# The second factor's way back from sums and differences of conjugate pairs, in 32x32 tiles of TensorE

## The chip, the cores and the metric

The kernel runs on one core of a Trainium2 chip. A core has TensorE (PE in the profile, with PEld for its weight loads), VectorE (DVE), ScalarE (ACT), GpSimd (POOL), SyncE (SP, which only issues transfers here) and 16 DMA engines. TensorE's 128x128 array can be used as smaller tiles that work side by side; it writes its results to PSUM, in banks of 128 partitions x 512 fp32 values. The metric is the time of one execution on the device in microseconds (us), the median of several runs.

## The reference, cut to what matters

```python
x: (8, 3008, 256);  filt_r, filt_i: (1505, 256)          # all fp32
X = np.fft.rfft(x, axis=1)                               # along the 3008 positions
Y = X * (filt_r + 1j * filt_i)[None]
y = np.fft.irfft(Y, n=3008, axis=1).astype(np.float32)   # (8, 3008, 256)
x = y.reshape(8 * 3008, 256)
h = x @ w_in                                             # 256 -> 2048
g = np.where(h > 0, h, np.exp(np.minimum(h, 0)) - 1)
out = g @ w_out                                          # 2048 -> 256
```

## The kernel before

The transform of length 3008 is done in two factors, 64 (with the twiddles in its tables) and 47. Rows n1 and 47 - n1 go together, so that 24 pairs stand for the 47. For each batch the stages are: `a_unit`, the first factor; `b_unit`, the way there of the second factor and the product with the filter; `bi_unit`, the way back of the second factor; `n_unit`, the way back of the first factor. Between the stages data go through DRAM (`z_write`, `z_read`, `y_write`, `y_read`) to be laid out anew. `b_unit` and `bi_unit` work in eight steps g of four values k2 each.

```python
def tile_mm(ps, table, k, rhs, special):
    for u, w, v in ((0, 1, 1), (1, 1, 0)) if special else ((0, 2, 0),):
        for n, r in enumerate(rhs):
            nc.tensor.matmul(ps[:, u:u + w, :], table[k, v, :], r[k, u:u + w, :], ...)   # L298

def b_unit(b, g, f=None, gb=gb, pq=None, between=None):
    ...
    (i0, re), (i1, im) = (bank(n) for n in ("psr", "psi"))
    for o, a in ((0, 0), (64, 2)):
        for ps, k in ((re, LO), (im, HI)):       # LO, HI: partitions 0-47 and 64-111
            tile_mm(ps[o:o + 64], gb, k, [t[:, a:a + 2, :]], g == 0 and a == 0)
    ...
    nc.vector.tensor_tensor(out=sr, in0=re, in1=f[:, 0], op=ALU.mult)
    nc.vector.tensor_tensor(out=si, in0=re, in1=f[:, 1], op=ALU.mult)
    nc.vector.scalar_tensor_tensor(out=p, in0=im, scalar=-1.0, in1=f[:, 1], op0=ALU.mult, op1=ALU.mult)
    nc.vector.tensor_tensor(out=q, in0=im, in1=f[:, 0], op=ALU.mult)
    banks.extend((i0, i1))
    ...                                          # batch 0 stops here: both parts go to bi_unit
    nc.gpsimd.tensor_tensor(out=sr, in0=sr, in1=p, op=ALU.add)
    nc.gpsimd.tensor_tensor(out=si, in0=si, in1=q, op=ALU.add)

def bi_unit(b, g):
    ...
    (i0, pa), (i1, pb) = (bank(n) for n in ("pva", "pvb"))     # for b > 0
    for o, table, sv in ((0, gr, s[0]), (64, gi, s[1])):
        for ps, k in ((pa, LO), (pb, HI)):
            tile_mm(ps[o:o + 64], table, k, sv, g == 0 and k == LO)
    nc.scalar.activation(out=t[:, 0:2, :], in_=pa, func=AXT.Copy)   # L337
    nc.scalar.activation(out=t[:, 2:4, :], in_=pb, func=AXT.Copy)   # L338
```

The two dense matrix products are done by a scheme that takes seven products of half-size blocks in place of eight. `up_steps` (L417, into the banks phs, pha, phd) and `down_steps` (L499, into four banks po of their own) are seven steps each of two matmuls of 128 rows and 128 columns. The main loop goes through 8 x 6 x 4 = 192 items ("quads"), and puts the units of the transform of the next batch into them, 24 quads to a batch:

```python
banks = [0, 1, 2, 3]                             # PSUM banks shared by all stages but po
PER = 24
for g in range(NG + 2):                          # NG = 8; t is the batch's first quad
    s = t + 9 + g
    if g >= 2: at(s, 1, bi_unit, b, g - 2)       # place 1: at the end of quad s
    if g < NG: at(s, 1, b_unit, b, g)
    if g >= 2: at(s, 1, y_write, b, g - 2)
...
for m, (s, place) in enumerate(((20, 0), (25, 1), (29, 1), (32, 0), (36, 0), (40, 0))):
    ...  at(t + s, place, n_unit, b, m)
...
for i in range(-PER, len(items) + 3):
    for k in "UUDUDDU": ...                      # one up or down step each
    for fn, a in plan.get((i, 0), ()): fn(*a)    # place 0
    for k in "DUUDUDD": ...
    ...                                          # the tails of the up and down steps
    for fn, a in plan.get((i, 1), ()): fn(*a)    # place 1
```

Batch 0 goes through the transform in an opening part of its own, ahead of the loop, with tables of its own (`once`).

Of the kernel before, what the change touches and what calls it, by code (L numbers as in the profile page):

```python
# [41 lines left out]
def _make_tables():  # L42
# [51 lines left out]
    gr[0:24, 1, 0:24], gr[24:48, 1, 24:48] = m0 * c0.T, m3 * c3.T  # L94
    gi[0:24, 1, 24:48], gi[24:48, 1, 0:24] = -m0 * s0.T, -m3 * s3.T
    lie = np.concatenate([2 * np.arange(24), 2 * np.arange(24) + 1])
    gb[:, :, lie] = gb[:, :, :48].copy()
# [6 lines left out]
    once = np.stack([np.eye(P), gf.reshape(P, P)], 1)  # L104
    return [t.astype(np.float32) for t in (ta, tn, np.stack([gb, gr, gi], 1), tf, once)]

# [7 lines left out]
def kernel(  # L114
# [10 lines left out]

    ta_d, tn_d, gs_d, tf_d, once_d = [
        nc.inline_tensor(t, name=n + "_t").ap()
        for t, n in zip(_make_tables(), ("ta", "tn", "gs", "tf", "once"))
    ]

    def pool(name, bufs, **kw):
        return ctx.enter_context(tc.tile_pool(name=name, bufs=bufs, **kw))
# [7 lines left out]
    t2p = pool("t2p", 2)  # L140
    sp = pool("sp", 2)
    qp = pool("qp", 1)
    t3p = pool("t3p", 2)
    t4p = pool("t4p", 2)
# [6 lines left out]

    gs = glob.tile([P, 3, 2, 64], FP32, name="gs")
    gb, gr, gi = (gs[:, i] for i in range(3))

# [3 lines left out]
    edges = glob.tile([P, 2], FP32, name="edges")  # L158
    fd = fdp.tile([NG, 2, 48, 2, 2, D], FP32, name="fd")

    xs, tas, tns, t1s, t2s, ss, t3s, t4s, zs, yds, ys, g_of, po_of, cs_, sds = ({} for _ in range(15))
# [127 lines left out]

    def f_read(b, g, t=None):  # L290
        t = fbufs[(b * NG + g) % FBUFS] if t is None else t
        for a, r in enumerate((LO, HI)):
            nc.gpsimd.dma_start(t[r].rearrange("p c u d -> p (c u d)"), fd[g, a].rearrange("q c u d -> q (c u d)"))

    def tile_mm(ps, table, k, rhs, special):
# [3 lines left out]

    def b_unit(b, g, f=None, gb=gb, pq=None, between=None):  # L300
        t = t2s.pop((b, g))
        f = fbufs[(b * NG + g) % FBUFS] if f is None else f
        (i0, re), (i1, im) = (bank(n) for n in ("psr", "psi"))
        for o, a in ((0, 0), (64, 2)):
            for ps, k in ((re, LO), (im, HI)):
                tile_mm(ps[o:o + 64], gb, k, [t[:, a:a + 2, :]], g == 0 and a == 0)
        if between:
            between()
        sr, si = (sp.tile([P, 2, D], FP32, tag=n, name=n) for n in ("sr", "si"))
        p, q = pq or (qp.tile([P, 2, D], FP32, tag=n, name=n) for n in ("sp", "sq"))  # L310

        nc.vector.tensor_tensor(out=sr, in0=re, in1=f[:, 0], op=ALU.mult)
        nc.vector.tensor_tensor(out=si, in0=re, in1=f[:, 1], op=ALU.mult)
        nc.vector.scalar_tensor_tensor(out=p, in0=im, scalar=-1.0, in1=f[:, 1], op0=ALU.mult, op1=ALU.mult)  # L314
        nc.vector.tensor_tensor(out=q, in0=im, in1=f[:, 0], op=ALU.mult)
        banks.extend((i0, i1))
        if b == 0:

            ss[b, g] = [sr, p], [si, q]
            return  # L320
        nc.gpsimd.tensor_tensor(out=sr, in0=sr, in1=p, op=ALU.add)  # L321
        nc.gpsimd.tensor_tensor(out=si, in0=si, in1=q, op=ALU.add)
        ss[b, g] = [sr], [si]

    def bi_unit(b, g):
        s = ss.pop((b, g))
        t = t3s[b, g] = t3p.tile([P, 4, D], FP32, tag="t3", name="t3")
        if b == 0:

            pa, pb = (psO.tile([P, 2, 256], FP32, tag="po%d" % i, name="po%d" % i)  # L330
                      for i in ((0, 1) if g > 2 and g % 2 else (2, 3)))
        else:
            (i0, pa), (i1, pb) = (bank(n) for n in ("pva", "pvb"))
        for o, table, sv in ((0, gr, s[0]), (64, gi, s[1])):
            for ps, k in ((pa, LO), (pb, HI)):
                tile_mm(ps[o:o + 64], table, k, sv, g == 0 and k == LO)
        nc.scalar.activation(out=t[:, 0:2, :], in_=pa, func=AXT.Copy)  # L337
        nc.scalar.activation(out=t[:, 2:4, :], in_=pb, func=AXT.Copy)  # L338
        if b > 0:
            banks.extend((i0, i1))  # L340

    def y_write(b, g, queues=(nc.sync, nc.sync)):
        if g == 0:
            yds[b] = yd.tile([K2, 96, D], FP32, tag="yd", name="yd")
        t = t3s.pop((b, g))
        for a, r in enumerate((LO, HI)):
            queues[a].dma_start(yds[b][4 * g:4 * g + 4, 48 * a:48 * a + 48, :].rearrange("u r d -> r u d"), t[r])

# [285 lines left out]
    def f_arrange():  # L634

        for c, src in enumerate((filt_r, filt_i)):
# [14 lines left out]
            nc.gpsimd.dma_start(fd[0, 0, 47:48, c, 1, :], raw(src, 4, [[D, 1], [1, D]]))  # L651

    with tc.manual_schedule():


        with tc.tile_pool(name="boot", bufs=1) as bp:
            ff = bp.tile([P, NG, 2, 2, D], FP32, name="ff")
            once = bp.tile([P, 2, P], FP32, name="once")
            eye, gf = once[:, 0], once[:, 1].rearrange("p (v q) -> p v q", v=2)
            pq = [bp.tile([P, 2, D], FP32, name="pq%d" % i) for i in range(2)]  # L660
            zt[0] += [bp.tile([P, 16 * ROWS], FP32, name="zt%d" % i) for i in range(2)]
# [50 lines left out]
            for g in range(NG):  # L712
                f_read(0, g, ff[:, g])
                if 3 <= g < 5:
                    w_fetch(g + 7)
# [6 lines left out]
            for g in range(NG + 2):  # L722
                back = (lambda g=g: bi_unit(0, g - 2)) if g >= 2 else None
                if g < NG:
                    b_unit(0, g, ff[:, g], gf, pq if g % 2 else None, back)
                else:
                    back()
                if g < 4:
                    t_first(g + 4)
                if g < 5:  # L730
                    w_float(g + 7)
                if g < 3:
                    w_join(g + 7)
                    w_split(g + 8)
                if g == 2:
                    w_split(11)
                if g >= 2:
                    y_write(0, g - 2, (nc.sync, nc.scalar if g == NG + 1 else nc.sync))
                if g == 7:
                    w_join(10)  # L740
                    w_join(11)
                    w_split(12)
                    w_split(13)
# [19 lines left out]
        PER = 24  # L763
        plan = {}

        def at(quad, place, fn, *a):
            plan.setdefault((quad, place), []).append((fn, a))
# [5 lines left out]
        for c in range(2, XBUFS):  # L773
            at(c - 2, 0, x_load, 1, c)
        for i, f in enumerate(fbufs):
            at(3 + i, 1, nc.vector.memset, f, 0.0)
        for b in range(B):
            t = (b - 1) * PER
            if b > 0:
                for c, s in enumerate((1 if b == 1 else 0, 2, 3, 4, 6, 7)):  # L780
                    at(t + s - 1, 0, x_unit, b, c)
                    at(t + s, 0, a_unit, b, c)
                    nb, nxt = (b, c + XBUFS) if c + XBUFS < NXC else (b + 1, c + XBUFS - NXC)
                    if nb < B:
                        at(t + s, 0, x_load, nb, nxt)
                    at(t + s, 0, z_write, b, c)
                for g in range(NG + 2):
                    s = t + 9 + g
                    if g >= 2:
                        at(s, 1, bi_unit, b, g - 2)  # L790
                    if g < NG:
                        at(s, 1, b_unit, b, g)
                    if g >= 2:
                        at(s, 1, y_write, b, g - 2)
                for g in range(NG):
                    s = t + 7 + g
                    at(s, 1, f_read, b, g)
                    at(s, 1, z_read, b, g)
            for m, (s, place) in enumerate(((20, 0), (25, 1), (29, 1), (32, 0), (36, 0), (40, 0))):
                if b > 0 or m > 0:  # L800
                    at(t + s - (1 if m == 0 else 2), 0, tn_read, b, m)
                    at(t + s - (1 if m == 0 else 2), 0, y_read, b, m)
                    at(t + s, place, n_unit, b, m)
                at(t + PER + 4 * m + 5, 0, c_unit, b, m)
                at(t + PER + 4 * m + 6, 0, o_unit, b, m)

        items = [(b, m, q) for b in range(B) for m in range(6) for q in range(4)]
        for i in range(-PER, len(items) + 3):
            ups, up_tail = up_steps(*items[i]) if 0 <= i < len(items) else ((), None)
            downs, down_tail = down_steps(*items[i - 1]) if 1 <= i <= len(items) else ((), None)  # L810
            ups, downs = list(ups), list(downs)
            for k in "UUDUDDU":
                s = ups if k == "U" else downs
                if s:
                    s.pop(0)()
            for fn, a in plan.get((i, 0), ()):
                fn(*a)
            for k in "DUUDUDD":
                s = ups if k == "U" else downs
                if s:  # L820
                    s.pop(0)()
# [38 lines left out]
```

## Time and profile before

| what | value |
|---|---|
| time, median of 3 runs | 2641.85 us (2640.01 to 2643.4) |
| span of the profiled execution | 2639.1 us |
| instructions | 37322 |
| TensorE clock granted, mean | 0.995 of full speed |
| first matmul of the main loop | 97 us after the span's start |
| DMA | 202.85 MB, mean 77 GB/s |

The busy share of an engine is the time in which it had an instruction running. Line numbers (L298) are those of the kernel before; a line in a helper, as L298, gathers all its callers, so tiles (psr, psi of `b_unit`; pva, pvb of `bi_unit`) tell them apart. The chain of work that ended last is followed back from the last instruction, and tells which engine's work the end had to wait for. Matmuls are pipelined, and the ends that the profile gives them are modelled; the distance of two starts is the surer measure.

### The profile page before, as it was taken

Reading aid. Unit: us, or ns where it says so; the run is one execution under the profiler, and the core shown is the slowest. Engines: PE = TensorE matmul, PEld = TensorE weight load, DVE = VectorE, ACT = ScalarE, POOL = GpSimd, SP = SyncE. Lnnn points to the kernel's source line nnn. Section 1 sums busy time; section 2 is a strip of 40 time slices with the busy share of each in tenths; the row PEclk is TensorE's granted clock in tenths of the full one; section 3 lists DMA queues with packets and bytes.
Section 4 is the critical chain, followed back from the end, with each engine's and each line's share of the span. In section 5 each row is a group of like instructions: output and inputs, shape, how many; then the busy total and the mean of one; then the engine's idle time right before and its main releaser. Section 6 shows DMA issues by size and latency. Waiting matters only on the chain.

```text
span 2639.1 us, 37322 instructions
## 1 busy us (share of the span) xinstructions
PE 2589.8 (98%) x13508; PEld 2208.4 (84%) x13508; DVE 1843.4 (70%) x3203; ACT 1508.0 (57%) x2622; POOL 236.7 (9%) x298
## 2 busy tenths in 40 slices
PE   5899999999999999999999999999999999999998
PEld 4688789887898888987889888988789887898887
DVE  6876766677666776677667676776767677666666
ACT  7655556555555555655555555555555555555554
POOL 5001200021000210002100020001200011000000
PEclk9999999999999999999999999999999999999999
DMA  9643313422233331424213341134321333110010
GB/s 292 151 104 88 86 34 76 114 75 75 52 92 79 90 73 39 103 73 103 72 37 87 93 111 45 39 92 105 98 50 43 81 78 81 38 41 19 22 28 17
DMA packets 224456, 202.85 MB, mean 77 GB/s; under 512 B 127586, under 2 KB 191090, under 8 KB 224272
## 3 DMA queue, kind: packets, MB, share of 16 engines
q1 hardware_dynamic: 211632, 166.70, 25.3%
q0 software_dynamic: 11184, 33.04, 4.9%
q8 instruction: 107, 1.75, 0.3%
q10 hardware_dynamic: 1456, 0.72, 0.1%
q14 instruction: 77, 0.63, 0.1%
HBM read 128.52 MB, written 74.97 MB: 77 GB/s over the span
## 4 chain that ended last, share of the span: by engine, by line
PE 97%; DMA 1%; DVE 1%; ACT 1%; issue 0%; SPq 0%; DVEq 0%; ACTq 0%
PE po L499 43%; PE phs L417 25%; PE phd L417 12%; PE pha L417 6%; PE psn L369 3%; PE pva L298 2%; PE psr L298 2%; PE psa L209 2%; DMA xc<-in_x_dram 1%; PE po L298 0%; PE psi L298 0%; PE pvb L298 0%; PE po L270 0%; DMA t<-yd 0%; PE psa L250 0%
## 5 line engine op out<-in xcount | busy, mean ns | idle before, releaser
L499 PE MATMUL po<-g,wo 128*128 128x256 f32 (+1 forms) x5376 | 1296.7, 375 | 0.0
L499 PEld LDWEIGHTS po<-g,wo 128*128 128x128 f32 x5376 | 1015.0, 190 | 129.5 <-issue 15.0
L428 ACT ACTIVATE g<-phs 128x512 f32<-128x512 f32 (+1 forms) x576 | 339.0, 589 | 842.7 <-PE phs L417 842.1
L425 DVE TENSOR_TENSOR g<-phd,g 128x512 f32<-128x512 f32 (+1 forms) x384 | 259.6, 676 | 457.2 <-ACT e L435 278.4
L435 ACT ACTIVATE e<-e 128x512 f32<-128x512 f32 (+1 forms) x768 | 477.3, 622 | 24.4
L417 PE MATMUL phs<-y,wi 128*128 128x256 f32 (+1 forms) x1536 | 395.2, 380 | 0.0
L417 PE MATMUL phs<-ys,wi 128*128 128x256 f32 (+1 forms) x1536 | 387.7, 375 | 0.7 <-ACT g L428 0.6
L439 DVE SCALAR_TENSOR_TENSOR g<-e,g 128x512 f32<-128x512 f32 (+1 forms) x576 | 387.1, 672 | 0.0
L434 ACT ACTIVATE e<-g 128x512 f32<-128x512 f32 (+1 forms) x576 | 352.7, 612 | 32.8 <-DVE g L425 28.1
L417 PEld LDWEIGHTS phs<-y,wi 128*128 128x128 f32 x1536 | 285.0, 190 | 83.2 <-ACT t L337 34.1
L417 PEld LDWEIGHTS phs<-ys,wi 128*128 128x128 f32 x1536 | 291.4, 190 | 34.6 <-ACT g L428 1.7
L439 DVE SCALAR_TENSOR_TENSOR g<-e,phs 128x512 f32<-128x512 f32 (+1 forms) x192 | 130.0, 677 | 138.6 <-ACT e L435 138.6
L417 PE MATMUL phd<-ys,wi 128*128 128x256 f32 (+1 forms) x768 | 193.8, 375 | 0.8 <-DVE g L425 0.8
L434 ACT ACTIVATE e<-phs 128x512 f32<-128x512 f32 (+1 forms) x192 | 113.0, 589 | 141.5 <-PE phs L417 140.6
L417 PE MATMUL phd<-y,wi 128*128 128x256 f32 (+1 forms) x768 | 193.7, 375 | 0.0
L417 PE MATMUL pha<-y,wi 128*128 128x256 f32 (+1 forms) x768 | 193.7, 375 | 0.0
L321 POOL TENSOR_TENSOR sr<-sr,sp 128x512 f32<-128x512 f32 x56 | 71.2, 1271 | 1246.3 <-DVE sp L314 1246.3
L417 PEld LDWEIGHTS phd<-ys,wi 128*128 128x128 f32 x768 | 145.7, 190 | 17.7 <-DVE g L425 1.1
L417 PEld LDWEIGHTS pha<-y,wi 128*128 128x128 f32 x768 | 145.8, 190 | 16.5
L417 PEld LDWEIGHTS phd<-y,wi 128*128 128x128 f32 x768 | 145.8, 190 | 16.5
L476 DVE TENSOR_TENSOR g<-g,g 128x512 f32<-128x512 f32 (+1 forms) x192 | 130.7, 681 | 6.7
L479 DVE TENSOR_TENSOR g<-g,g 128x512 f32<-128x512 f32 (+1 forms) x192 | 130.7, 681 | 6.6
(133 smaller groups left out, 2343.9 us busy)
## 6 DMA issues: line engine op xcount, KB each, us to landing
yd<-t SPq DMA_DIRECT2D x127, 192.0 KB
t<-yd SPq DMA_DIRECT2D x190, 128.0 KB
z<-t SPq DMA_DIRECT2D x84, 256.0 KB
f<-fd POOLq DMA_DIRECT2D x112, 192.0 KB, 3.6
t<-z SPq DMA_DIRECT2D x224, 96.0 KB
out_dram<-o SPq DMA_DIRECT2D x632, 32.0 KB
tn<-tn_t SPq DMA_DIRECT2D x48, 256.0 KB
xc<-in_x_dram SPq DMA_DIRECT2D x84, 128.0 KB
```

Source lines behind the costliest of these rows:

```text
L298: nc.tensor.matmul(ps[:, u:u + w, :], table[k, v, :], r[k, u:u + w, :], start=n == 0, stop=n == len(rhs) - 1)
L321: nc.gpsimd.tensor_tensor(out=sr, in0=sr, in1=p, op=ALU.add)
L369: nc.tensor.matmul(ps[:, ts(q, P)], t[:, i - 4 * m, ds(dh * P, P)], w[:, i - 4 * m, :], start=True, stop=True)
L417: nc.tensor.matmul(ps[:, a, 0:h], w_in[q][:, COMBO[n], a, :], y[n], start=start and a == 0, stop=True, skip_group_check=True)
L425: nc.vector.tensor_tensor(out=g[o], in0=i0, in1=i1, op=ALU.add)
L428: nc.scalar.activation(out=g[o], in_=i0, func=AXT.Copy)
L434: nc.scalar.activation(out=e, in_=src, func=AXT.Relu, scale=-1.0)
L435: nc.scalar.activation(out=e, in_=e, func=AXT.Exp, scale=-1.0)
L439: nc.vector.scalar_tensor_tensor(out=g[n], in0=es[n], scalar=1.0, in1=src, op0=ALU.subtract, op1=ALU.max)
L476: nc.vector.tensor_tensor(out=b12, in0=b22, in1=b12, op=ALU.subtract)
L479: nc.vector.tensor_tensor(out=g["t4"], in0=g["b21"], in1=g["t2"], op=ALU.subtract)
L499: nc.tensor.matmul(po[i][:, u, 0:h], w_out[q][:, COMBO[n], a, :], g[n][:, a, :], start=q == 0 and a == 0 and n in (1, 3, 6, 4), stop=True, ...
```

## The change

For batches 1 to 7 the second factor is laid out by pairs. Each of a step's four values k2 gets 32 partitions of its own, of which 24 are used, and the two members of a conjugate pair of frequencies stand side by side in the two halves of a PSUM bank. `b_unit` writes that layout with 16 matmuls of 32 columns of the array. GpSimd then forms, after the two additions, the sum and the difference of each pair, for the real and the imaginary part. With these the way back needs four tables of 24x24 (the cosine or sine half each) where it had two of 48x48. `bi_unit` takes two steps at once, as 32 matmuls on sixteen 32x32 tiles, into all four shared banks. Batch 0 keeps the old form (`b_first`, `bi_first`, `y_write_first`), and the filter is once arranged anew in DRAM (`f_pairs`) for the others. The aim is less work on TensorE for the way back. The diff, cut to its core:

```diff
-    sp = pool("sp", 2)
-    qp = pool("qp", 1)
-    t3p = pool("t3p", 2)
+    sp = pool("sp", 1)
+    qp = pool("qp", 2)
+    t3p = pool("t3p", 1)
...
+    def f_read(b, g):
+        t = fbufs[(b * NG + g) % FBUFS]
+        for a in range(4):
+            nc.gpsimd.dma_start(t[32 * a:32 * a + 24]..., fp[g, a]...)
...
+    def b_unit(b, g):
+        ...
+        for c in range(2):
+            for a in range(4):
+                for ps, k in ((re, LO), (im, HI)):
+                    nc.tensor.matmul(ps[32 * a:32 * a + 32, c, :], fb[k, 1 if g == a == 0 else 0, c, :], t[k, a, :],
+                                     start=True, stop=True)
+        ...
+        products(re, im, f, sr, si, p, q)        # the four products on VectorE, as before
+        banks.extend((i0, i1))
+        nc.gpsimd.tensor_tensor(out=sr, in0=sr, in1=p, op=ALU.add)
+        nc.gpsimd.tensor_tensor(out=p[:, 0], in0=sr[:, 0], in1=sr[:, 1], op=ALU.add)
+        nc.gpsimd.tensor_tensor(out=p[:, 1], in0=sr[:, 0], in1=sr[:, 1], op=ALU.subtract)
+        nc.gpsimd.tensor_tensor(out=si, in0=si, in1=q, op=ALU.add)
+        nc.gpsimd.tensor_tensor(out=q[:, 0], in0=si[:, 0], in1=si[:, 1], op=ALU.subtract)
+        nc.gpsimd.tensor_tensor(out=q[:, 1], in0=si[:, 0], in1=si[:, 1], op=ALU.add)
+        if g == 0:
+            nc.gpsimd.tensor_copy(out=p[0:32], in_=sr[0:32])
+            for i in range(2):
+                nc.gpsimd.tensor_copy(out=q[0:32, i], in_=si[0:32, 1 - i])
...
+    def bi_unit(b, g):
+        s = [ss.pop((b, g + j)) for j in range(2)]
+        t = t3s[b, g] = t3p.tile([P, 2, 4, D], FP32, tag="t3", name="t3")
+        pv = [bank("pv") for _ in range(4)]
+        for j in range(2):
+            for p in range(4):
+                for a, (_, ps) in enumerate(pv):
+                    r = slice(32 * a, 32 * a + 24)
+                    nc.tensor.matmul(ps[32 * p:32 * p + 32, j, :], bb[r, 1 if g + j == a == 0 else 0, p, :], s[j][p][r],
+                                     start=True, stop=True, tile_position=(32 * a, 32 * p))
+        for a, (i, ps) in enumerate(pv):
+            nc.scalar.activation(out=t[:, :, a, :], in_=ps, func=AXT.Copy)
+            banks.append(i)
...
+                for g in range(NG):
+                    s = t + 9 + g + g // 2
+                    at(s, 1, b_unit, b, g)
+                    at(s - 2, 1, f_read, b, g)
+                    at(s - 2, 1, z_read, b, g)
+                    if g % 2:
+                        opens.add(s + 2)
+                        at(s + 1, 1, bi_unit, b, g - 1)
+                        at(s + 1, 1, y_write, b, g - 1)
-            for m, (s, place) in enumerate(((20, 0), (25, 1), ...
+            for m, (s, place) in enumerate(((23, 0), (25, 1), ...
...
-            for k in "UUDUDDU":
+            for k in "DUUDUDDU" if i in opens else "UUDUDDU":
...
-            for k in "DUUDUDD":
+            for k in "DUUDUD" if i in opens else "DUUDUDD":
```

## The prediction before the run

> **What bounds the kernel now.** I read the page first: busy shares, then the chain that ended last.
>
> ```profile
> PE 2589.8 (98%) x13508; PEld 2208.4 (84%) x13508; DVE 1843.4 (70%) x3203; ACT 1508.0 (57%) x2622; POOL 236.7 (9%) x298
> ...
> PE 97%; DMA 1%; DVE 1%; ACT 1%; issue 0%; SPq 0%; DVEq 0%; ACTq 0%
> ```
>
> TensorE (PE) is busy 98% of the span and is 97% of the chain. After the opening part the loop has 192 items ("quads") of 56 dense 128-row matmul instructions each; each matmul in the source shows as two instructions (5376 at L499 are 192 x 14 x 2). Whatever time a transform unit takes between two quads adds to the end one for one; whatever the other engines gain is worth nothing by itself. So the question is what one unit costs on PE. The timeline of PE around a quad's end shows it: columns are start, length, engine, line, operation, operands, form, count.
>
> ```profile
> 595.42 1.03 PE L417 MATMUL phd<-ys,wi 128*128 128x256 f32 x4
> 596.28 1.89 PE L499 MATMUL po<-g,wo 128*128 128x256 f32 x8
> 598.10 0.64 PE L298 MATMUL pva<-sr,gs 48*64 48x512 f32 x1
> 598.11 0.64 PE L298 MATMUL pvb<-sr,gs 48*64 48x512 f32 x1
> 598.12 0.64 PE L298 MATMUL pva<-si,gs 48*64 48x512 f32 x1
> 598.12 0.64 PE L298 MATMUL pvb<-si,gs 48*64 48x512 f32 x1
> 598.58 0.59 PE L298 MATMUL pva<-sr,gs 48*64 48x512 f32 x1
> ...
> 599.44 0.59 PE L298 MATMUL psr<-t,gs 48*64 48x512 f32 x1
> ...
> 599.98 1.13 PE L417 MATMUL phs<-y,wi 128*128 128x256 f32 x4
> 600.95 1.03 PE L417 MATMUL pha<-y,wi 128*128 128x256 f32 x4
> ```
>
> Four dense instructions take 0.864 us (595.42 to 596.28), so 0.216 us each. Four 48x64 instructions start within 0.02 us of each other and run side by side, one on each quarter of the array; the next four start 0.43 us later (599.01 to 599.44, rounds of 512 columns). A unit, way there (psr, psi) or way back (pva, pvb), is two such rounds, 0.86 us. From 596.28 to 600.95 are 4.67 us; the 12 dense instructions in it account for 12 x 0.216 = 2.59; the pair of units cost 2.08 us. A lone way-back unit near the end of the transforms:
>
> ```profile
> 2252.21 1.89 PE L499 MATMUL po<-g,wo 128*128 128x256 f32 x8
> ...
> 2255.05 1.13 PE L417 MATMUL phs<-y,wi 128*128 128x256 f32 x4
> 2256.02 1.03 PE L417 MATMUL pha<-y,wi 128*128 128x256 f32 x4
> ```
>
> 3.81 - 2.59 = 1.22 us, and the same view at 220.04 to 223.86 gives 1.23 for a lone way-there unit. So: 0.86 us a unit, and **0.36 us for each visit** to the small tiles, in which the array goes out of the 128-row form and back. In a batch the schedule has 2 quads with a way-there unit alone, 6 with both, 2 with a way-back unit alone: 2 x 1.22 + 6 x 2.08 + 2 x 1.22 = 17.4 us; seven batches run through the loop (batch 0 runs in the opening part, whose form the change keeps): **122 us**, 4.6% of the span. This is all that the change can touch on the path.
>
> **What the Trainium skill says.** (1) TensorEngine Tiling (Array Packing), Key Properties: changing the tiling mode drains TensorE, and tiles run independently. The trace agrees: 0.36 us per visit, and tiles side by side. (2) TensorE: Matmul & The Clock Gate, Measured speedup vs the span model: 16 tiles of 32x32 gave 10.6 times one, with about 4 ns per tile on top. The trace has only four tiles, 7 ns apart (598.10 to 598.12); nothing here shows sixteen, nor this in fp32. (3) The same page, "Wait — 56ns, not 53.3ns?": start-to-start never below some 25 ns, and 62 ns per matmul where the sequencer decodes in software. The trace contradicts a 25 ns floor for short groups on different tiles (7 ns), but shows no long one. (4) TensorEngine Tiling, Gotcha 1: different row tiles have to write different PSUM banks. Hence the four banks at once; before, two row tiles used two.
>
> **The change, part by part**, per batch of the loop.
>
> *Way back, PE.* Eight units of 8 instructions become four units of two steps, each 32 matmuls, 64 instructions of 256 columns. Sixteen run side by side, so four rounds. A 256-column round is 0.216 us (the 128-row instruction above; the 64x64 group psa at 419.66, 419.87, 420.09 shows the same 0.21 to 0.22). Four rounds are 0.86 us: for two steps what one cost before. Removed: 4 x 0.86 = 3.4 us.
>
> *Way there, PE.* The table now fills 32 columns of the array per matmul and each of the four k2 has its own 32 partitions of the output: 16 matmuls, 32 instructions of 256 columns, eight tiles at once, four rounds: 0.86 us again, no gain. It only pays for the layout that the way back needs.
>
> *Visits.* Units no longer share a visit: 8 + 4 = 12 quads in place of 10. Added: 2 x 0.36 = 0.7 us. A longer group also takes longer to start and to drain, 7 ns a tile: 4 more tiles x 8 and 12 more x 4 are 80 x 7 ns = 0.6 us.
>
> *Sum.* 3.4 - 0.7 - 0.6 = 2.1 us a batch; times 7, **15 us**. 2642 - 15 = 2627.
>
> *GpSimd.* It makes the sums and differences.
>
> ```profile
> L322 POOL TENSOR_TENSOR si<-si,sq 128x512 f32<-128x512 f32 x56 | 73.3, 1308 | 0.0
> L321 POOL TENSOR_TENSOR sr<-sr,sp 128x512 f32<-128x512 f32 x56 | 71.2, 1271 | 1246.3 <-DVE sp L314 1246.3
> ```
>
> Two adds of 1.3 us become these two and four of half the length, which I estimate at half, 0.65 us: 2.6 + 2.6 = 5.2 us, about 7 in step 0 with its three copies. They begin after VectorE's products, some 3 us after the unit on PE (in this stage sp starts at 602.31 and GpSimd at 603.08), and the way back reads them a quad later, 13 to 14 us on. 3 + 5 = 8, so there are 5 us of slack; the single sr and si buffer needs the same and has it.
>
> *ScalarE.* Two copies of 128x512 for each step stay two for each step (0.6 us long, 0.5 apart: L337 at 627.62, L338 at 628.11); they now come four in a row, so the last bank is free some 2.2 us after the matmuls, not 1.1. Now the first phs after a pair of units starts when the copy ends:
>
> ```profile
> L337 ACT ACTIVATE t<-pva x56: 597/598/601, 249.6 to 2268.5; 128x512 f32<-128x512 f32 x56
> ...
> who waited for it (us, times):
>   PEld phs L417: 34.1, 42
> ```
>
> These 34 us are not lost: a lone way-there unit, with no copy to wait for, costs the same 1.22. In the changed kernel the quad after a way back starts with a down step (psO banks, 0.86 us), then two up steps. If the matmuls end at T, the first up step comes at T + 1.1 and its bank is free at about T + 0.75; the second bank at T + 1.25, needed at T + 1.9; the keep copy queues to T + 2.25, and its next user comes at T + 2.8 or later, as one more down step lies between. It fits, with some 0.3 us to spare. Before the way back all four banks must be free. The last of them is phd:
>
> ```profile
> 624.98 0.68 DVE L425 TENSOR_TENSOR g<-phd,g 128x512 f32<-128x512 f32 x1
> ...
> 626.42 0.13 PEld L298 LDWEIGHTS pva<-sr,gs 48*64 48x64 f32 x1 [0.33 <-issue]
> ```
>
> It is read by 625.66, and the unit starts at 626.42: 0.76 us of slack.
>
> *DMA.* The bytes per batch stay; the filter is read in four pieces for two (192 KB became 96 KB each), and it is rearranged once in DRAM, in early quads without such reads. With a DMA share of 0.3 through most of the loop and two quads of lead, I give it nothing. The opening part keeps its double buffers: 0. The first tile of the way back of the first factor moves from quad 20 to 23, half a quad before its first use; its copies and combination need 3 to 4 us of the 6.5: 0.
>
> **The rivals.** *A, issue becomes the bound.* The densest long group in the trace is psa, 16 instructions with their weight loads in four rounds of 0.21, 54 ns each. 64 instructions in 0.86 us are 13 ns each, 32 are 27. The 7 ns of neighbouring tiles speaks for it being possible, but may only be what a filled queue gives out. If 54 ns is what the sequencer sustains, a way back takes 3.4 us and a way there 1.7: 4 x 2.6 + 8 x 0.86 = 17 us a batch, 120 us in all: about 2747. *B, more than two tiles on the same rows take turns.* Today each row group feeds two column tiles; the change asks for four. If the rounds double in the way back alone: 4 x 0.86 x 7 = 24 us, 2651; in both, 72 us, 2699. Point 2 of the skill speaks against it, though at other data types. *C, the four banks.* If each way back makes PE wait 1 us, before (VectorE late with phd) or after (ScalarE's four copies), 28 us: 2655. The slack of 0.76 and 0.3 us speaks against most of it. *D, GpSimd late* would stop PE by microseconds; 5 us of slack speak against.
>
> **Range and chances.** PE's arithmetic is the surest part: the sums of the trace reproduce to hundredths from quad to quad. I take 2627. The low end, 2612, is no dispatch cost and no waits, with half of the visits cheaper than I think; even taking the whole way back out (6 x 0.86 + 2 x 1.22 = 7.6 us a batch, 53 in all) would only just reach 2%, so faster by over 2% has 0.02. The high end, 2655, is B for the way back or C in full. Slower by over 2% (2695) needs A or the double form of B: 0.07. Within: 0.91.
>
> **What would show it.** Right: way-back rounds 0.21 to 0.22 us apart with 16 starts in each; a lone unit 1.2 to 1.35 us by the sum above; 12 visits a batch; no wait of PE on the four copies; GpSimd at about 5 us a step and still waiting for VectorE. Wrong: instructions of the way back spread evenly at 25 ns or more (A); rounds 0.43 apart (B); phs waiting for copies or the unit waiting for VectorE (C).

## The result and the profile after

The changed kernel takes 2653.53 us (median of 4 runs, 2652.82 to 2654.75), the kernel before 2642.62 in the same comparison: ratio 1.0042, 95% interval 1.0025 to 1.0059. It is slower by 0.4%, where 0.6% faster was predicted. The page of the changed kernel, the lines that answer to those of before:

```profile
PE 2593.1 (98%) x16140; PEld 2228.4 (84%) x16140; DVE 1860.2 (70%) x3203; ACT 1507.0 (57%) x2622; POOL 488.8 (18%) x669
...
PE 91%; DVE 2%; ACT 1%; SPq 1%; DMA 1%; issue 1%; DVEq 0%; ACTq 0%
```

PE still bounds, but its share of the chain fell from 97% to 91%: other engines now stand in the chain, so PE waits for them somewhere. The span grew by 11.7 us. The starts of the matmuls divide it: up to the first up step +3.2 us (97.2 to 100.3), from there to the last down step +9.3 (2532.4 to 2541.7), the rest -0.8. In the loop, adding up the distances of starts beyond the dense 0.216 us gives this account of the 9.3:

| in the loop, us | before | after | difference |
|---|---|---|---|
| units of way there and way back, with their visits | 121.4 | 114.4 | -7.0 |
| phd late (after po), 20 times | 0 | 7.5 | +7.5 |
| psn late (after phs), 7 times | 0 | 6.1 | +6.1 |
| second matmul after a wait, mostly 0.1 each | 1.8 | 4.4 | +2.6 |

A lone way-there unit costs 1.22 us in all 56 places, as the old one. The way back of two steps costs 1.65 in 21 of 28 places and 1.62 in seven. PE's timeline of one:

```profile
614.50 0.44 PE L401 MATMUL pv<-sp,pairs 24*32 24x256 f32 x8
614.55 0.45 PE L401 MATMUL pv<-sq,pairs 24*32 24x256 f32 x8
614.74 0.42 PE L401 MATMUL pv<-sp,pairs 24*32 24x256 f32 x8
614.79 0.42 PE L401 MATMUL pv<-sq,pairs 24*32 24x256 f32 x8
614.96 0.69 PE L401 MATMUL pv<-sp,pairs 24*32 24x256 f32 x9
615.29 0.48 PE L401 MATMUL pv<-sq,pairs 24*32 24x256 f32 x6
...
615.53 0.49 PE L401 MATMUL pv<-sq,pairs 24*32 24x256 f32 x8
615.95 1.13 PE L565 MATMUL po<-g,wo 128*128 128x256 f32 x4
```

The first 32 instructions are as predicted: sixteen start within 0.1 us, 7 ns apart, the next sixteen 0.24 us after them. The 33rd starts at 614.96. The 34th follows only 0.19 us later, and from there one starts about every 17 ns; the last starts 1.146 us after the first, where four rounds would have ended their starts at some 0.77 (an estimate from the rounds and the 7 ns above). The other two losses stand in the waits (engine, what waited, for what: us in total, times, longest):

```profile
PEld phd L483 <- DVE g L491: 13.3, 21, 1.0
...
PE psn L435 <- DMA t<-yd: 13.3, 6, 9.9
...
PE phd L483 <- DVE g L491: 5.0, 14, 0.7
```

In before each of the two phd lines is one single wait, of 1.1 and 0.8 us. A wait of PEld, the weight load, can begin while PE still works, and PE's ends are modelled, so the table's 7.5 us, from the starts, is the surer figure. Of the psn line, 9.9 us is the one wait at the end of the opening part, which before has as well (9.8).

### The profile page after: what moved, and what is told of

The parts are those of the page before. It is cut to its first block, busy times and chain, and to the rows that moved or that the text cites. A ratio compares the mean times of both kernels' runs of the same rounds, so it can differ in the third digit from the quotient of the medians.

```text
span 2650.8 us, 42967 instructions
## 1 busy us (share of the span) xinstructions
PE 2593.1 (98%) x16140; PEld 2228.4 (84%) x16140; DVE 1860.2 (70%) x3203; ACT 1507.0 (57%) x2622; POOL 488.8 (18%) x669
## 4 chain that ended last, share of the span: by engine, by line
PE 91%; DVE 2%; ACT 1%; SPq 1%; DMA 1%; issue 1%; DVEq 0%; ACTq 0%
PE po L565 41%; PE phs L483 24%; PE phd L483 12%; PE pha L483 6%; PE psn L435 3%; PE psr L372 2%; PE psa L226 2%; PE pv L401 2%; DMA t<-yd 1%; SPq L613 1%; DVE g L491 0%; ACT e L501 0%; ACT g L494 0%; ACT e L500 0%; DVE ys L460 0%
## 5 line engine op out<-in xcount | busy, mean ns | idle before, releaser
L491 DVE TENSOR_TENSOR g<-phd,g 128x512 f32<-128x512 f32 (+1 forms) x384 | 259.6, 676 | 439.7 <-ACT e L501 259.3
L505 DVE SCALAR_TENSOR_TENSOR g<-e,g 128x512 f32<-128x512 f32 (+1 forms) x576 | 400.6, 695 | 1.7 <-ACT e L501 1.1
L505 DVE SCALAR_TENSOR_TENSOR g<-e,phs 128x512 f32<-128x512 f32 (+1 forms) x192 | 129.7, 676 | 116.2 <-ACT e L501 116.2
L491 DVE TENSOR_TENSOR g<-pha,g 128x512 f32<-128x512 f32 (+1 forms) x192 | 129.1, 673 | 29.5 <-PE pha L483 29.5
L542 DVE TENSOR_TENSOR g<-g,g 128x512 f32<-128x512 f32 (+1 forms) x192 | 130.7, 681 | 6.7
```

The costliest lines, as they stand in the source:

```text
L491: nc.vector.tensor_tensor(out=g[o], in0=i0, in1=i1, op=ALU.add)
L505: nc.vector.scalar_tensor_tensor(out=g[n], in0=es[n], scalar=1.0, in1=src, op0=ALU.subtract, op1=ALU.max)
L542: nc.vector.tensor_tensor(out=b12, in0=b22, in1=b12, op=ALU.subtract)
```

## Experiments

Each run is compared with the kernel before on the same chip: its median was 2642.62 us beside after, 2644.62 beside a1 to a4, and 2644.36 beside a5, a7 and b1. So runs of different groups are compared by their ratios or loops, not by their times. "Loop" is the time from the first up step's first matmul to the start of the last matmul in that run's trace; "start" is when the first up step begins.

| run | time, us | ratio to before, interval | start | loop |
|---|---|---|---|---|
| before; a second trace of it | 2642.62; 2643.21 | 1 | 97.2; 99.3 | 2532.4; 2532.7 |
| after | 2653.53 | 1.0042 [1.0025, 1.0059] | 100.3 | 2541.7 |
| a1_cols512 | 2651.83 | 1.0029 [1.0018, 1.0040] | 100.9 | 2540.1 |
| a2_yread | 2648.67 | 1.0016 [1.0008, 1.0023] | 101.5 | 2537.1 |
| a3_order | 2647.86 | 1.0012 [1.0005, 1.0019] | 101.0 | 2536.1 |
| a4_nosum (leaves work out) | 2654.70 | 1.0042 [1.0025, 1.0059] | 98.7 | 2544.6 |
| a5_normal | 2665.22 | 1.0078 [1.0065, 1.0092] | 102.1 | 2554.2 |
| a7_xmove | 2642.92 | 0.9995 [0.9987, 1.0003] | 100.4 | 2531.6 |
| b1_all | 2630.32 | 0.9951 [0.9937, 0.9964] | 95.7 | 2521.2 |

### a1_cols512: half as many instructions for the same tiles

The sums of both steps lie in one tile, twice as large and with one buffer where there were two, so that a matmul takes both at once.

```diff
-        for j in range(2):
-            for p in range(4):
-                for a, (_, ps) in enumerate(pv):
-                    nc.tensor.matmul(ps[32*p:32*p+32, j, :], bb[...], s[j][p][r], ...)
+        for p in range(4):
+            for a, (_, ps) in enumerate(pv):
+                for j, w, v in ((0, 1, 1), (1, 1, 0)) if g == a == 0 else ((0, 2, 0),):
+                    nc.tensor.matmul(ps[32*p:32*p+32, j:j+w, :], bb[r, v, p, :], s[r, p, j:j+w, :], ...)
```

> The way back of two steps as 16 matmuls of 512 columns in place of 32 of 256: same tiles, same columns streamed, half the instructions (32 in place of 64; 40 in the first unit of a batch, whose tables differ). Theory Q (the first 32 instructions of a unit come out of a filled queue 7 ns apart, the rest only after a gap of 0.19 us and 17 ns apart): the gap and the slow second half go, a unit falls from 1.65 to about 1.30 us, 28 units, so about 10 us less than the changed kernel: 2644 us. Rival T (sixteen tiles hinder each other in the array or in the banks): a unit stays at 1.6 us or more and the time at 2653.

PE's timeline, a unit of 32 instructions, and then the first unit of a batch with 40:

```profile
615.52 1.14 PE L403 MATMUL pv<-pq,pairs 24*32 24x512 f32 x32
616.59 1.13 PE L567 MATMUL po<-g,wo 128*128 128x256 f32 x4
```

```profile
572.50 2.14 PE L403 MATMUL pv<-pq,pairs 24*32 24x256 f32 x40
574.57 1.13 PE L567 MATMUL po<-g,wo 128*128 128x256 f32 x4
```

From the unit's first matmul to the next dense one it is 1.07 us with 32 instructions and 1.45 with 64 (614.50 to 615.95). By the sum used in the prediction a unit costs 1.27 us in 21 of 21 places. Sixteen tiles stream 512 columns side by side without hindering each other, so T falls, and Q holds for them. But the 7 units with 40 instructions cost 2.26 us, worse than with 64: the 34th load comes 0.56 us after the first, and the next three only at 0.65, 0.86 and 1.08. In the units with 64 the 34th comes at 0.46 and the 35th again at 0.65 (all 28). So in both the stop comes at the same count, 34 loads, and ends at the same time. It does not come from loading a tile more than twice: a way-there unit gives each of its eight tiles four loads in 32 instructions, and its rounds start 0.24, 0.46 and 0.67 us after the first, without a gap. That 40 cost more than 64 the count does not explain; in the 40, two different tables follow each other on the same tile, and no run separates the two. What happens in the stop the trace does not show. The 21 units gave back 7.8 us, the 7 took 4.3, and psn waited 1.7 longer in that run, so the time fell by little.

### a2_yread: the read ahead of the stores

```diff
-                    at(t + s - (1 if m == 0 else 2), 0, y_read, b, m)      # m == 0: middle of quad 22
+                    at(t + s - 2, 1 if m == 0 else 0, y_read, b, m)        # m == 0: end of quad 21
```

(and tn_read likewise.)

> The read of yd for the first tile of the first factor's way back goes from the middle of quad 22 to the end of quad 21, ahead of the output stores of that quad on the same queue. Theory S (the read stands behind 16 stores which wait for VectorE's transposes): the 7 waits of psn (0.3 to 1.6 us, 6.1 in all) and the phd waits of 0.43 us in the same quad 23 (7 with what follows, 3.7 us) go, about 9 us less than the changed kernel: 2644 us. Rival D (the data are not there earlier, as the way back's writes land late): psn still waits and the time stays at 2653.

The reason for it, in the timeline of SyncE's queue and then of PE in the changed kernel:

```profile
716.55 8.47 SPq L613 DMA_DIRECT2D out_dram<-o  x16
725.06 0.43 SPq L417 DMA_DIRECT2D tn<-tn_t  x1
725.53 1.82 SPq L422 DMA_DIRECT2D t<-yd  x4
```

```profile
728.52 1.03 PE L483 MATMUL phs<-ys,wi 128*128 128x256 f32 x4
731.00 1.69 PE L435 MATMUL psn<-tn,t 128*128 128x128 f32 x13 [1.45 <-issue]
```

Quad 22 is also one in which the 16 stores of an output tile are issued, 8.5 us of issue time on the one queue, ahead of the four reads. The last writes of the rows they read had been issued from 701 to 704. In the kernel before, this read was issued in quad 19, which has no such stores. In a2_yread the psn waits are gone, all 7; S is right, D is not. PE at that place, with nothing between phs and psn:

```profile
729.58 1.03 PE L483 MATMUL phs<-ys,wi 128*128 128x256 f32 x4
730.44 1.95 PE L435 MATMUL psn<-tn,t 128*128 128x128 f32 x16
```

But phd's wait in the same quad 23 grew from 0.43 to 0.80 us, so that only half of the gain came out, 4.6 us of the loop. VectorE there:

```profile
734.11 0.39 DVE L461 TENSOR_TENSOR ys<-y,ys 128x224 f32<-128x224 f32 x1
734.42 0.68 DVE L214 TENSOR_TENSOR sd<-xc 128x512 f32<-128x512 f32 x1
735.13 0.69 DVE L215 TENSOR_TENSOR xc<-xc 128x512 f32<-128x512 f32 x1
735.74 0.68 DVE L491 TENSOR_TENSOR g<-phd,g 128x512 f32<-128x512 f32 x1
```

VectorE has the next batch's x_unit (L214, L215) queued ahead of the addition that frees phd. These waits are six, not seven: in the last batch no x_unit follows, and there phd does not wait.

### a7_xmove: x_unit out of the way

```diff
-                    at(t + s - 1, 0, x_unit, b, c)
+                    at(t + s - 1, 1 if c == 0 else 0, x_unit, b, c)
```

> As a2_yread, and besides the sums and differences of the next batch's first input tile on VectorE (x_unit, two operations of 0.68 us) go from the middle of quad 23 to its end. Theory X (tile combination and x_unit fall together on VectorE in the middle of quad 23 and make phd late by 0.80 us): the 7 waits go, 6 us less than a2_yread: 2643 us. Rival (the combination alone is what is late): the waits stay above 0.4 us and the gain is under 3 us.

The time is 2642.92 us, and the loop is 5.5 us shorter than in a2_yread: the waits of quad 23 are gone, X is right. PE at that place:

```profile
732.59 1.03 PE L565 MATMUL po<-g,wo 128*128 128x256 f32 x4
733.45 1.03 PE L483 MATMUL phd<-ys,wi 128*128 128x256 f32 x4
```

Exactly dense, 0.86 apart. What is left is the 14 waits of phd of 0.16 and 0.54 us in other quads (4.9 us).

### a3_order: fewer up steps late

```diff
-            for k in "DUUDUDDU" if i in opens else "UUDUDDU":
+            for k in "DUUDUDU" if i in opens else "UUDUDDU":
...
-            for k in "DUUDUD" if i in opens else "DUUDUDD":
+            for k in "DUUDUDD":
```

> In the quads after a way back the steps go D U U D U D U | D U U D U D D: only the first three up steps come later than in a normal quad, not all seven. Theory O (the late last up step leaves VectorE's tail late for the next quad, so that phd waits in the quad after): the waits of phd of 0.16 and 0.54 us in 13 quads go, with the slow restart 0.1 each, 6 us less than the changed kernel: 2647 us. Rival G (GpSimd's sums slow VectorE there): the waits stay, 2653.

The waits of 0.16 and 0.54 us are gone, 4.9 us; the six of quad 23 stay, as they should. A new small one came: the fourth up step now follows the third after only one down step, and there are 28 more waits of 0.09 us between phs matmuls, 2.6 us. The loop is 5.6 us shorter, of which 3.2 are psn waits that happened to be shorter in this run. So the order does remove these waits, as O says, and nets 2.4 us.

### a4_nosum: without GpSimd's sums and differences

```diff
-        nc.gpsimd.tensor_tensor(out=p[:, 0], in0=sr[:, 0], in1=sr[:, 1], op=ALU.add)
-        nc.gpsimd.tensor_tensor(out=p[:, 1], in0=sr[:, 0], in1=sr[:, 1], op=ALU.subtract)
```

(and the two for q; the way back then works on the products alone.)

> Leaves out the four half-size sums and differences on GpSimd (the way back then works on the unsummed products). Theory G: VectorE's two-input operations beside GpSimd go back from 0.95 to 0.68 us and the phd waits of 0.16 and 0.54 us in 13 quads go: 2647 us. Rival O (order of the up steps): VectorE is faster, but more than half of these waits stays: 2650 to 2653.

The suspicion came from VectorE's timeline in the changed kernel, while GpSimd made its sums (594.45 to 600.7):

```profile
597.67 0.68 DVE L491 TENSOR_TENSOR g<-phd,g 128x512 f32<-128x512 f32 x1
598.27 1.16 DVE L505 SCALAR_TENSOR_TENSOR g<-e,g 128x512 f32<-128x512 f32 x1
```

Beside GpSimd's operations the second of these (L505), with both inputs in SBUF, took 0.95 us in the mean of 49, and 0.68 elsewhere; L491, with one input in PSUM, stayed at 0.68 to 0.69. Without the sums all of L505 are at 0.68. The 0.54 us waits are gone too: in that quad VectorE combines a tile of the first factor's way back beside the sums, and from its first operation to the one that frees phd it is 2.55 us with them and 1.67 without. But in the quad that had waited 0.16 us phd now waits 0.56, 7 times: GpSimd's second addition comes earlier there and beside another of VectorE's two-input operations, which took 1.38 us where the changed kernel has 0.84. In sum 3.9 us of 4.9 stay, and psn waited 9.6 us for 6.1, so that the time did not fall. Neither theory holds alone: the late up steps leave VectorE no slack, and what GpSimd then adds to it decides in which quad PE waits and for how long. Either the order (a3) or, in the one quad, the sums' absence removes the wait. In a3_order L505 at this place is as slow as in the changed kernel, 1.15 us, and phd does not wait, so the slowing alone does not stop PE there.

### a5_normal: the normal order of steps after a way back

```diff
-            for k in "DUUDUDDU" if i in opens else "UUDUDDU":
+            for k in "UUDUDDU":
...
-            for k in "DUUDUD" if i in opens else "DUUDUDD":
+            for k in "DUUDUDD":
```

> The changed kernel with the normal order of steps everywhere (no down step first after a way back). Theory O: phd no longer waits in 13 quads (6.4 us with the slow restart), but the first up step stands right behind the way back and waits for ScalarE's copies of the four banks: 0.5 to 1.0 us in each of 28 quads, 14 to 28 us. In sum 8 to 20 us more than the changed kernel: 2661 to 2673 us. Rival: the copies are early enough and the order is needless: 2647.

The time is 2665.22 us. The 14 waits of phd are gone, as O expected, but behind each way back the first up step waits for the copies; the unit with its following wait costs 2.38 us for 1.65, 20.5 us in all. In the waits:

```profile
PEld phs L483 <- ACT t L404: 32.1, 28, 1.1
```

So the down step first is worth 20 us; its side effect on the next quads costs 6.

### b1_all: all four repairs

a1 (with the first unit of a batch left at 64 instructions), a2, a7 and a3 together.

> All repairs at once: 512 columns for the way back of two steps (the first unit of a batch keeps 64 instructions of 256), the read of yd a half quad earlier, x_unit of the first input tile at the end of quad 23, and the order D U U D U D U | D U U D U D D after a way back. If the losses found so far are separate: 21 x 0.38 = 8.0, psn and phd of quad 23 together 10, order 5, in all 23 us less than the changed kernel: 2630 us, 0.5% under the kernel before. If VectorE is what limits these quads and repairs only move the wait: 2638 or more.

The time is 2630.32 us; ratio to before 0.9951, interval 0.9937 to 0.9964. In the loop no wait of psn or phd over 0.06 us is left. The page:

```profile
PE 2580.3 (98%) x15468; PEld 2210.0 (84%) x15468; DVE 1858.8 (71%) x3203; ACT 1502.8 (57%) x2622; POOL 482.7 (18%) x669
```

PE's units cost 68.4 (way there) + 26.6 + 11.4 (way back) = 106.4 us, for 121.4 before. The losses were separate ones, and the change beats the kernel before once they are gone. The loop is 20.5 us shorter than in the changed kernel and 11.2 shorter than in before. The other part of the profiled run's gain is its early start, 95.7, which none of the repairs was meant to bring; the five times spread from 2627.59 to 2635.03, so that 2630.32 meets the expected 2630 so closely by luck.

### before_again: the opening part

> The kernel before, unchanged, for a second look at its opening part. In the five traces of the changed kernel and its variants TensorE's granted clock is 0.50 around 73 to 76 us, and the first up step starts at 98.7 to 101.5 us; in the one trace of before the clock is 1.00 there and the first up step starts at 97.2. If that is chance of the clock's timing, this trace may show the low clock there too and a start near 100; if the change causes it, again 97.

Here the clock was 0.50 from 65 to 70 us and 1.00 at 73 to 76, and the first up step started at 99.3. In seven of the eight traces of the changed kernel and its variants the clock fell to about 0.5 between 70 and 79 us, where PE was busy nearly throughout, and the start was at 98.7 to 102.1; in b1_all it was 1.00 from 70 to 82 and the start 95.7. So start and clock go together over a few microseconds, also where the opening part's code is the same (97.2 and 99.3 for before) or nearly so (95.7 to 102.1 for the eight). That the clock is the cause is not shown. Whether the change makes the low clock there more likely stays open; it may be 1 to 3 of the 11 us.

## Why the prediction was wrong, step by step

The measured 2653.5 us lies inside the stated range only by luck: its end at 2655 was worked out for rival B or C in full, and neither came. The forecast direction, 15 us faster, was wrong.

- *What bounds*: right. PE still sets the end, and each wait put on it added one for one.
- *Way there*: right; 1.25 predicted, 1.22 measured (56 times, 1.6 us in all to the good). *Visits*: right; 12 a batch, 0.36 each. *Tiles side by side* (rival B): right, sixteen do run at once.
- *Way back, PE* was the first term mis-sized: "four rounds are 0.86 us". With its visit and dispatch 1.30 was predicted and 1.65 measured, 28 times, **9.6 us**. It is rival A in part: the issue does become the bound, but only for what lies beyond some 32 instructions. I had written that the 7 ns "may only be what a filled queue gives out", but took the issue as all fast (7 ns) or all slow (54 ns, 2747 us), and not as fast for the first half of a unit alone. a1 showed it by halving the count.
- *DMA*, "two quads of lead, I give it nothing", and the tile moved to quad 23, "0", failed. The moved tile's read has one quad of lead, not two (`1 if m == 0` in a2's edit), and the lead was counted in quads, not on the queue: the reads are issued in order behind 16 stores. And quad 23 has x_unit on VectorE. Cost: 6.1 of psn + 2.6 of phd + about 1.2 for restarts, **10 us**; a2 and a7 took 10.1 us out of the loop.
- *ScalarE and the four banks* (rival C): the working for the quad after a way back was right (the copies fit, and a5 shows 20 us if they don't). It failed at the end of that quad: all up steps come one place later, VectorE's tail with them, and phd is late one quad on. GpSimd's slowing of VectorE has its part in it. 4.9 us of waits and 1.5 of restarts, **6 us**; with a3 the waits are gone, at 2.6 us of new small ones.
- *GpSimd*: the time was 0.74 to 0.93 us in the mean for each half-size operation, not 0.65, and the slack was enough, as predicted. That it slows VectorE was not foreseen, though the trace of before has a case: its L515, c<-c,k, took 1.37 us beside GpSimd's additions and 0.43 elsewhere (14 and 26 times).

The sum: -15.1 - 1.6 + 9.6 + 10 + 6 = +9, as against the 9.3 measured in the loop. The opening part's 3 us were predicted as 0.

## What to carry to other kernels

When a matmul is cut into many small tiles, count the instructions of a burst as well as its columns: here a burst of 32 cost what its columns say, 64 cost 0.4 us more and 40, in another order, 1 us more, while the same tiles with twice the columns each got the gain. When a stage moves to another slot in a tightly packed schedule, look at what is queued ahead of it on each in-order queue of that slot (stores before a read, another stage's additions before the one that frees a bank), since PE at 97% of the chain pays for every such wait. And try the repairs of a change that lost little: a loss of 0.4% was here three losses over a gain of 0.5%.

## What the runs showed of the hardware that was not expected

- In a burst of 64 matmul instructions on sixteen tiles, the 33rd was followed by 0.19 us without a start, and then one started about every 17 ns, in place of every 7 ns (28 of 28 units). The 35th weight load came 0.65 us after the first, in bursts of 64 and of 40 alike.
- A burst of 40 instructions, in which two different tables follow each other on four of the sixteen tiles, took 2.26 us; 64 with the tiles in turn took 1.65.
- VectorE's operation L505, with both inputs in SBUF, took 0.95 us in the mean, up to 1.22, beside GpSimd's additions and 0.68 elsewhere; GpSimd's half-size additions took up to 1.26 for 0.73. VectorE's operations with one input in PSUM were not slowed (0.68 to 0.69).
- A second matmul after a wait of PE started 0.1 us later than a dense one, so each short wait costs 0.1 us more than its length.
